# Backward of single-query attention on one core: scores as 512-column matmuls with q among 32 weights, and eight stores that leave out two DMA engines

## The chip, the core and the metric

The kernel runs on one core of one Trainium2 chip. The metric is the device time of one execution in microseconds, as the median of several runs; 1287.31 us before the change (five runs, 1287.27 to 1288.17). The profile shows one execution of the same program. The core has TensorE (PE, with its weight loads PEld), VectorE (DVE), ScalarE (ACT), GpSimd (POOL) and SyncE (SP), and sixteen DMA engines that all transfers share.

## The reference

For 64 heads (2 x 32), each with one query q of 128 numbers and 8,192 rows of k and v, all bf16, the reference computes the attention output and its gradients. In short, per head:

```
s  = (k . q) / sqrt(128)          8192 scores
p  = softmax(s)
out = p . v                        out_0
dp = v . grad_out                  8192
ds = p * (dp - sum(p * dp)) / sqrt(128)
dq = ds . k                        out_1
dk = ds outer q                    out_2, 8192 x 128
dv = p outer grad_out              out_3, 8192 x 128
```

So k and v of every head are read once (268 MB in all) and dk and dv are written once (268 MB). The scores of a head are 8,192 dot products with q for k, and as many with grad_out for v.

## The kernel before

**Tiles.** The k or the v of one head is one SBUF tile `kvt` of 2 MB: 128 partitions, each with NT = 64 rows of 128 numbers (16 KB per partition). There are NTILE = 12 such tiles, so six heads are in the core at a time. `outer` writes dk and dv over k and v in the same tile; the tile is stored from there, and when the store has landed, the load of the head six further on takes the place (`slot_of`, AHEAD = 6). Loads are issued from SP (`load`, L98), stores from POOL (L412, and L87 for the heads in SPREAD); only the last head is stored in four pieces per tile, from SP.

**Steps.** The main loop (L423) goes through steps of one chunk: 16 of the 64 rows per partition. A head has SL = 8 chunks, NCH = 4 of k and then 4 of v, and a new head begins every eight steps. The work of one head stretches over some 17 steps, so that up to three heads are in work at a time; `at(r)` and `within(r)` pick the head that stands at its step r. Every instruction is pinned (`pin`), so the order of the loop body is the order on each engine.

In a step, PE transposes the 16 blocks of the chunk with an identity into PSUM (L184, `tp`), and ACT copies them to SBUF (L186, `ev`). In the next step PE multiplies each transposed block as weights by the column q or grad_out (L195): sixteen matmuls with one moving column, each of which fills one column of `sw` (k) or `dpw` (v). That gives the scores with rows on the partitions. From there:

- r = 4: `max_part` takes the maximum per partition on DVE (L207); r = 5: `max_all` transposes it and reduces again (L211, L213); r = 6: `max_spread` brings it to all partitions (L218, L228), and `expo` computes the exponentials on ACT (L238); DVE casts them into `E_pad` (L247).
- r = 7: `normalise_p` sums (L282), takes the reciprocal and makes pairs of p (L291, L270, L295).
- r = 8: `weigh` computes the sum of p times dp (L253); r = 9: `normalise_ds` makes ds, `dS_pad` and its pairs (L305 to L270).
- r = 8 to 11 (`acc`, w = 1) and 12 to 15 (w = 0): p . v and ds . k as matmuls with 64 weights and 512 moving columns, in two halves of the array (L339); r = 12 and 16: `pick` (L356, L362) takes the wanted blocks out of the sum on DVE, and two steps later `join` adds them (L376, L379).
- r = 9 to 12 and 13 to 16: `outer` writes dv and dk, one chunk per step (L394, DVE); after the fourth chunk the tile is stored.

In steps r = 3 and r = 6, `broadcast` spreads grad_out and q over the partitions (L168 on PE, L177 on DVE).

**PSUM.** `sw` holds the scores of k, the transposed maximum and its broadcast; `dpw` holds those of v, two sums and the broadcast q (`qbp`). Each is one bank and there is one of each.

**Spread stores.** A store of 128 rows (one per partition) gives each of the sixteen DMA engines eight. The dk of the heads in SPREAD goes out as two stores instead, of 126 and of 2 rows (`by_rows`):

```python
SPREAD = range(5, 64, 9)
            if w == 0 and i in SPREAD:
                by_rows(store_eng, dst, h.tile[w], (P - 2, 2))
```

[...]

Of the kernel before, what the change touches and what calls it, by code (L numbers as in the profile page):

```python
# [11 lines left out]
BF16 = mybir.dt.bfloat16  # L12
F32 = mybir.dt.float32

CH = 16
QT = 4
CW = 64
NG = 2
NTILE = 12
FIRST = 6  # L20
SPREAD = range(5, 64, 9)


@with_exitstack
def kernel(
# [11 lines left out]
    nc = tc.nc  # L37
    B, H, Sq, D = q.shape
    Sk = k.shape[2]
    P = nc.NUM_PARTITIONS  # L40
    assert Sq == 1 and D == P
    BH = B * H
    assert BH <= P
    NT = Sk // P
    assert NT * P == Sk and NT % CH == 0
    NCH = NT // CH
    SL = 2 * NCH
# [4 lines left out]
    pin = tc.keep_in_program_order  # L52

    const = ctx.enter_context(tc.tile_pool(name="const", bufs=1))
    kvp = ctx.enter_context(tc.tile_pool(name="kv", bufs=1))
    evp = ctx.enter_context(tc.tile_pool(name="ev", bufs=2))
    work = ctx.enter_context(tc.tile_pool(name="work", bufs=1))
    small = ctx.enter_context(tc.tile_pool(name="small", bufs=2))
    ps_tp = ctx.enter_context(tc.tile_pool(name="ps_tp", bufs=2, space=bass.MemoryType.PSUM))
    ps_sdp = ctx.enter_context(tc.tile_pool(name="ps_sdp", bufs=1, space=bass.MemoryType.PSUM))  # L60
# [15 lines left out]
    heads = [Head() for _ in range(BH)]  # L76

    def slot_of(i, w):

        n = 2 * i + w  # L80
        return n if n < NTILE else slot_of(i - NTILE // 2, 1 - w)

    def by_rows(eng, dst, src, rows):

        p = 0
        for m in rows:
            pin(eng.dma_start(out=dst[p : p + m], in_=src[p : p + m], max_dma_last_dim=NT * D))  # L87
            p += m

    def load(i, w, pieces=(NCH,)):  # L90
        h = heads[i]
        t = kvp.tile([P, NT, D], BF16, tag=f"kv{slot_of(i, w)}", name="kvt")
        h.tile[w] = t
        src = (v_v if w else k_v)[i]
        c = 0
        for m in pieces:
            n0, n1 = c * CH, (c + m) * CH
            pin(load_eng.dma_start(out=t[:, n0:n1, :], in_=src[:, n0:n1, :]))  # L98
            c += m
# [4 lines left out]
    for w, a in enumerate((q, grad_out)):  # L104
        rows = a.rearrange("b h s d -> (b h s) d")
        r0 = FIRST if w == 0 else 0
        if r0:
# [3 lines left out]
                    out=qd_nat[:r0, w, :], in_=rows[:r0], max_dma_last_dim=D  # L111
# [4 lines left out]
    load(0, 1)  # L116
    for j in range(1, min(NTILE // 2, BH)):
        load(j, 0)
# [4 lines left out]
    ident_f = const.tile([P, P], F32)  # L123
    masks.make_identity(nc, ident_f[:])
    ones = const.tile([P, 1], F32)
    nc.vector.memset(ones[:], 1.0)
    groups = [g * P // NG for g in range(NG)]
    diag = const.tile([P, QT], F32)
# [7 lines left out]
    nc.vector.memset(E_pad[:], 0.0)  # L136
    nc.vector.memset(dS_pad[:], 0.0)

    qdT = const.tile([P, 2, BH], BF16)
    for w in range(2):  # L140
        tps = ps_m.tile([P, BH], BF16, tag=f"acc{w}", name="tps")
        nc.tensor.transpose(tps[:], qd_nat[:BH, w, :], ident_bf[:BH, :BH])
        nc.vector.tensor_copy(out=qdT[:, w, :], in_=tps[:])

    dqT = const.tile([P, BH], BF16)
    oT = const.tile([P, BH], BF16)

    def begin_s(i):

        h = heads[i]  # L150
        sw = ps_sdp.tile([P, NT + P + 1], F32, tag="s", name="sw")
        h.s = sw[:, 0:NT]
        h.mT = sw[0:1, NT : NT + P]
        h.mb = sw[:, NT + P :]

    def begin_dp(i):

        h = heads[i]
        dpw = ps_sdp.tile([P, NT + 2 + D], F32, tag="dp", name="dpw")
        h.dp = dpw[:, 0:NT]  # L160
        h.lsum = dpw[:, NT : NT + 2]
        h.qbp = dpw[:, NT + 2 :]

    def broadcast(i, w):

        h = heads[i]
        pin(
            nc.tensor.matmul(  # L168
                h.qbp,
                lhsT=qdT[:, w, i : i + 1].to_broadcast([P, P]),  # L170
                rhs=ident_bf[:],
                start=True,
                stop=True,
            )
        )
        h.qb[w] = small.tile([P, D], BF16, tag=f"qb{w}", name="qb")
        pin(nc.vector.tensor_copy(out=h.qb[w][:], in_=h.qbp))  # L177
# [9 lines left out]
        return ev  # L187

    def score_chunk(i, c, ev):
        h = heads[i]  # L190
        w, c = divmod(c, NCH)
        dst = h.dp if w else h.s
        for t in range(CH):
            pin(
                nc.tensor.matmul(  # L195
                    dst[:, c * CH + t : c * CH + t + 1],
                    lhsT=ev[:, t, :],
                    rhs=qdT[:, w, i : i + 1],
                    start=True,
                    stop=True,  # L200
                )
            )

    def max_part(i):
        h = heads[i]
        h.mp = small.tile([P, 1], F32, tag="mp", name="mp")
        pin(nc.vector.reduce_max(out=h.mp[:], in_=h.s, axis=AX.X))  # L207

    def max_all(i):
        h = heads[i]  # L210
        pin(nc.tensor.transpose(h.mT, h.mp[:], ident_f[:]))  # L211
        h.gm = small.tile([1, 1], F32, tag="gm", name="gm")
        pin(nc.vector.reduce_max(out=h.gm[:], in_=h.mT, axis=AX.X))  # L213
# [114 lines left out]
    def acc(i, w, c):  # L328
# [6 lines left out]
        for m in range(CH // QT):  # L335
            n0 = c * CH + m * QT
            g = groups[m % NG]
            pin(
# [3 lines left out]
                    rhs=rows[:, n0 : n0 + QT, :].rearrange("p n d -> p (n d)"),  # L342
                    start=(c == 0 and m < NG),
                    stop=(c == NCH - 1 and m >= CH // QT - NG),
                )
# [42 lines left out]
    def outer(i, w, c, ends):  # L388

        h = heads[i]  # L390
        n0 = c * CH
        shape = [P, CH, D // 2, 2]
        pin(
            nc.vector.tensor_tensor(  # L394
                out=h.tile[w][:, n0 : n0 + CH, :].rearrange("p n (e t) -> p n e t", t=2),
                in0=h.qb[w][:]
                .rearrange("p (e t) -> p e t", t=2)
                .unsqueeze(1)
                .to_broadcast(shape),
                in1=h.pair[w][:, n0 : n0 + CH, :].unsqueeze(2).to_broadcast(shape),  # L400
                op=ALU.mult,
            )
        )
        if c + 1 in ends:
            at = ends.index(c + 1)
            b0, b1 = (ends[at - 1] if at else 0) * CH, (c + 1) * CH
            dst = (dv_v if w else dk_v)[i]
            if w == 0 and i in SPREAD:
                by_rows(store_eng, dst, h.tile[w], (P - 2, 2))
            else:  # L410
                eng = load_eng if len(ends) > 1 else store_eng
                pin(eng.dma_start(out=dst[:, b0:b1, :], in_=h.tile[w][:, b0:b1, :]))  # L412
# [6 lines left out]
    last = list(range(1, NCH + 1))  # L419
    AHEAD = NTILE // 2  # L420

    prev = None
    for g in range(SL * BH + O0 + NCH + 4 - SL):  # L423
        now = [(g // SL - b, g % SL + b * SL) for b in range(4)]
        now = [(i, r) for i, r in now if 0 <= i < BH]

        def at(r0):

            return next((i for i, r in now if r == r0), None)

        def within(r0):

            return next(((i, r - r0) for i, r in now if r0 <= r < r0 + NCH), None)

        if (i := at(O1 + NCH)) is not None and i + AHEAD < BH:
            load(i + AHEAD, 0)
        if (i := at(O0 + NCH)) is not None and i + AHEAD < BH:
            load(i + AHEAD, 1)
        if x := within(O1):
            outer(x[0], 1, x[1], last if x[0] == BH - 1 else whole)  # L440
        if x := within(O0):
            outer(x[0], 0, x[1], last if x[0] == BH - 1 else whole)
        ev = None
        if g < SL * BH:
            i, r = divmod(g, SL)
            if r == 0:
                begin_s(i)
            if r == 3:
                begin_dp(i)
                broadcast(i, 1)  # L450
            if r == 6:
                broadcast(i, 0)
            ev = transpose_chunk(i, r)
        if (i := at(A1 + NCH + 2)) is not None:
            join(i, 1)
        if (i := at(A0 + NCH + 2)) is not None:
            join(i, 0)
        if x := within(A1):
            acc(x[0], 1, x[1])
        if x := within(A0):  # L460
            acc(x[0], 0, x[1])
        if (i := at(NCH + 2)) is not None:
            max_spread(i)
            expo(i)
        if prev is not None:
            score_chunk(*prev)
        prev = (g // SL, g % SL, ev) if ev is not None else None

        if (i := at(NCH)) is not None:
            max_part(i)  # L470
        if (i := at(NCH + 1)) is not None:
            max_all(i)
        if (i := at(NCH + 3)) is not None:
            normalise_p(i)
        if (i := at(SL)) is not None:
            weigh(i)
        if (i := at(SL + 1)) is not None:
            normalise_ds(i)
        if (i := at(A1 + NCH)) is not None:
            pick(i, 1)  # L480
        if (i := at(A0 + NCH)) is not None:
            pick(i, 0)

    for w, (src, dst) in enumerate(((dqT, out_1), (oT, out_0))):
        tps = ps_m.tile([BH, P], BF16, tag=f"acc{w}", name="tps")
# [34 lines left out]
```

## Time and profile before

| What | us |
|---|---|
| median of five runs | 1287.31 |
| the profiled execution, its own time | 1287.31 |
| its span, first to last instruction | 1285.5 |
| busy PE / PEld / DVE / ACT | 1127.2 / 857.7 / 935.7 / 975.9 |
| L195, matmuls of the scores, k / v: busy | 141.8 / 140.7 |
| L195, their weight loads: busy | 243.1 |
| L207, the maximum: idle of DVE before it | 152.2 |
| stores of 2,048 KB (POOL), issue to landing | 67.0 |
| loads of 2,048 KB (SP), issue to landing | 20.9 and 20.8 |
| mean granted clock of TensorE | 0.96 |

In the profile an engine's busy time is the union of its instructions; a matmul's end is modelled. Idle time stands before the group that followed it, with the instruction that ended most of it. DMA queue q1 is SP's, q0 POOL's, and q8 brings instructions. Read the queues as shares of the time of all sixteen DMA engines.

### The profile page before, as it was taken

Reading aid. Unit: us, or ns where it says so; the run is one execution under the profiler, and the core shown is the slowest. Engines: PE = TensorE matmul, PEld = TensorE weight load, DVE = VectorE, ACT = ScalarE, POOL = GpSimd, SP = SyncE. Lnnn points to the kernel's source line nnn. Section 1 sums busy time; section 2 is a strip of 40 time slices with the busy share of each in tenths; the row PEclk is TensorE's granted clock in tenths of the full one; section 3 lists DMA queues with packets and bytes.
Section 4 is the critical chain, followed back from the end, with each engine's and each line's share of the span. In section 5 each row is a group of like instructions: output and inputs, shape, how many; then the busy total and the mean of one; then the engine's idle time right before and its main releaser. Section 6 shows DMA issues by size and latency. Waiting matters only on the chain.

```text
span 1285.5 us, 42575 instructions
## 1 busy us (share of the span) xinstructions
PE 1127.2 (88%) x19268; PEld 857.7 (67%) x19268; DVE 935.7 (73%) x2122; ACT 975.9 (76%) x641; POOL 75.3 (6%) x142
## 2 busy tenths in 40 slices
PE   6999999988898988989888898889888998988880
PEld 5777777766676666766666676667666776766650
DVE  2888888777687777767776776768677777677781
ACT  6888888877787777877777787778777787777750
POOL 0000000000000000000000000000000000000000
PEclk9999999999999999999999899999899999899985
DMA  9999999999999999999999999999999999999995
GB/s 387 422 427 427 427 426 428 427 428 426 428 428 427 427 428 427 420 429 427 429 426 425 425 427 427 427 427 424 428 428 427 426 425 424 428 427 427 425 397 225
DMA packets 39986, 539.68 MB, mean 420 GB/s; under 512 B 5116, under 2 KB 5116, under 8 KB 6396
## 3 DMA queue, kind: packets, MB, share of 16 engines
q1 hardware_dynamic: 20172, 272.70, 49.9%
q0 software_dynamic: 19632, 264.25, 48.7%
q8 instruction: 150, 2.46, 0.7%
q14 instruction: 32, 0.26, 0.0%
HBM read 268.47 MB, written 268.47 MB: 418 GB/s over the span
## 4 chain that ended last, share of the span: by engine, by line
DMA 36%; PE 27%; another core or an unknown queue 19%; DVE 11%; issue 3%; ACT 1%; SPq 1%; POOL 0%; DVEq 0%; ACTq 0%; POOLq 0%
DMA kvt<-in_v_dram 26%; PE tp L184 12%; PE acc L339 7%; DVE kvt L394 6%; DMA kvt<-in_k_dram 5%; DMA out_dram<-kvt 4%; PE dpw L195 4%; PE sw L195 3%; DVE sel L362 2%; ACT ev L186 1%; PE dpw L282 1%; SPq L98 1%; DVE sel L356 1%; DMA qd_nat<-in_q_dram 1%
## 5 line engine op out<-in xcount | busy, mean ns | idle before, releaser
L186 ACT COPY ev<-tp 128x2048 bf16<-128x2048 bf16 x512 | 955.0, 1866 | 265.3 <-PE tp L184 253.6
L184 PE MATMUL tp<-ident_bf,kvt 128*128 128x128 bf16 x8192 | 557.3, 223 | 95.9 <-DMA kvt<-in_v_dram 73.9
L394 DVE TENSOR_TENSOR kvt<-qb,pair 128x2048 bf16<-128x2048 bf16 x512 | 621.9, 1215 | 0.2
L184 PEld LDWEIGHTS <-kvt 128*128 128x128 bf16 x8192 | 488.8, 100 | 102.6 <-DMA kvt<-in_v_dram 77.6
L195 PEld LDWEIGHTS <-ev 128*128 128x128 bf16 x8192 | 243.1, 96 | 208.2 <-issue 148.9
L339 PE MATMUL acc<-kvt,dS_pad 128*64 128x512 bf16 x1024 | 167.4, 409 | 0.8 <-DVE dqT L379 0.8
L339 PE MATMUL acc<-kvt,E_pad 128*64 128x512 bf16 x1024 | 160.5, 394 | 0.0
L195 PE MATMUL dpw<-qdT,ev 128*128 128x1 bf16 x4096 | 140.7, 164 | 17.8 <-DVE qb L177 17.0
L362 DVE SCALAR_TENSOR_TENSOR sel<-acc,diag,sel 128x128 f32<-128x128 f32 x384 | 134.7, 351 | 13.6
L195 PE MATMUL sw<-qdT,ev 128*128 128x1 bf16 x4096 | 141.8, 164 | 1.2 <-ACT ev L186 1.2
L412 POOL DMA_DIRECT2D out_dram<-kvt x119 | 64.0, 537 | 1089.4 <-DVE kvt L394 984.5
L207 DVE TENSOR_REDUCE mp<-sw 128x1 f32<-128x64 f32 x64 | 14.4, 225 | 152.2 <-PE sw L195 152.2
L339 PEld LDWEIGHTS <-dS_pad 128*64 128x64 bf16 x1024 | 37.5, 110 | 24.4 <-issue 5.1
L247 DVE CAST E_pad<-E_f 128x64 bf16<-128x64 f32 x64 | 12.5, 196 | 55.4 <-ACT E_f L238 55.4
L339 PEld LDWEIGHTS <-E_pad 128*64 128x64 bf16 x1024 | 36.4, 108 | 21.3 <-issue 0.7
L376 PE MATMUL acc<-ones,sel 128*128 128x1 f32 x256 | 43.5, 239 | 6.2 <-DVE sel L362 6.2
L253 DVE CUSTOM_DVE_ANT_0 junk<-E_f,dpw 128x64 bf16<-128x64 f32 x64 | 14.2, 221 | 45.5 <-PE dpw L195 45.5
L282 PE MATMUL dpw<-ld,ones 128*128 128x1 f32 x256 | 46.3, 250 | 0.1
L356 DVE TENSOR_SCALAR sel<-acc,diag 128x128 f32<-128x128 f32 x128 | 44.2, 345 | 0.0
L376 PEld LDWEIGHTS acc<-ones,sel 128*128 128x128 f32 x256 | 39.2, 194 | 7.3 <-DVE sel L362 7.3
L177 DVE CAST qb<-dpw 128x128 bf16<-128x128 f32 x128 | 35.6, 278 | 6.2 <-PE dpw L168 6.2
L282 PEld LDWEIGHTS dpw<-ld,ones 128*128 128x128 f32 x256 | 38.2, 188 | 0.5 <-DVE ld L253 0.5
(44 smaller groups left out, 313.5 us busy)
## 6 DMA issues: line engine op xcount, KB each, us to landing
out_dram<-kvt POOLq DMA_DIRECT2D x119, 2048.0 KB, 67.0
kvt<-in_v_dram SPq DMA_DIRECT2D x64, 2048.0 KB, 20.9
kvt<-in_k_dram SPq DMA_DIRECT2D x63, 2048.0 KB, 20.8
out_dram<-kvt POOLq DMA_DIRECT2D x7, 2016.0 KB, 70.3
out_dram<-kvt SPq DMA_DIRECT2D x8, 512.0 KB, 24.1
kvt<-in_k_dram SPq DMA_DIRECT2D x2, 512.0 KB, 4.5
kvt<-in_k_dram SPq DMA_DIRECT2D x1, 1024.0 KB, 7.1
out_dram<-kvt POOLq DMA_DIRECT2D x7, 32.0 KB, 70.3
```

Source lines behind the costliest of these rows:

```text
L177: pin(nc.vector.tensor_copy(out=h.qb[w][:], in_=h.qbp))
L184: pin(nc.tensor.transpose(tp[:, t, :], src[:, c * CH + t, :], ident_bf[:]))
L186: pin(nc.scalar.copy(out=ev[:], in_=tp[:]))
L195: nc.tensor.matmul(dst[:, c * CH + t : c * CH + t + 1], lhsT=ev[:, t, :], rhs=qdT[:, w, i : i + 1], start=True, stop=True,)
L207: pin(nc.vector.reduce_max(out=h.mp[:], in_=h.s, axis=AX.X))
L282: nc.tensor.matmul(out, lhsT=ones[:].to_broadcast([P, P]), rhs=col, start=True, stop=True)
L339: nc.tensor.matmul(h.acc[w][g : g + CW, :], lhsT=wts[:, n0 : n0 + CW], rhs=rows[:, n0 : n0 + QT, :].rearrange("p n d -> p (n d)"), start=( ...
L356: nc.vector.tensor_scalar(out=h.sel[:], in0=block, scalar1=diag[:, 0:1], scalar2=None, op0=ALU.mult)
L362: nc.vector.scalar_tensor_tensor(out=h.sel[:], in0=block, scalar=diag[:, b : b + 1], in1=h.sel[:], op0=ALU.mult, op1=ALU.add,)
L376: nc.tensor.matmul(h.acc[w][:, 0:1], lhsT=h.sel[:], rhs=ones[:], start=True, stop=True)
L394: nc.vector.tensor_tensor(out=h.tile[w][:, n0 : n0 + CH, :].rearrange("p n (e t) -> p n e t", t=2), in0=h.qb[w][:] .rearrange("p (e t) -> ...
L412: pin(eng.dma_start(out=dst[:, b0:b1, :], in_=h.tile[w][:, b0:b1, :]))
```

## The change

Two edits.

**Spread stores.** SPREAD goes from seven heads (5, 14, ... 59) to eight (4, 11, ... 53).

**Scores.** The transposed chunk `ev` becomes the moving operand, and q a column among 32 weights. q and grad_out of head i stand in `qdT` at column Q0 + 4i, with zeros between; chunk c takes the 32 columns that begin c before it, so that q is weight c of the 32 and the others are zero. Four matmuls of 512 columns, one for each quarter of the array's columns, write four groups of 32 partitions of a new PSUM tile `raw`; the four chunks of k (then of v) are added up in it, so that partition 32g + c holds the scores of quarter g of chunk c. `keep_raw` copies `raw` to SBUF on DVE, and `spread_rows` brings the scores back to rows on partitions with four fp32 matmuls by a selection `sel4`. `sw` and `dpw` become one tile, in one bank. max_part, max_all, max_spread, expo, normalise_p, weigh and normalise_ds stand one step later than before; acc, outer, pick, join, loads and stores keep their steps. broadcast of grad_out goes from r = 3 to r = 4.

```diff
-SPREAD = range(5, 64, 9)
+SG = 4
+SW = 32
+SPREAD = range(4, 60, 7)
...
+    sel4 = const.tile([P, NCH, SG], F32)
+    nc.vector.memset(sel4[:], 0.0)
+    for g in range(SG):
+        nc.vector.tensor_copy(
+            out=sel4[g * SW : (g + 1) * SW, :, g],
+            in_=ident_f[g * SW : (g + 1) * SW, g * SW : g * SW + NCH],
+        )
+
+    Q0 = NCH - 1
+    qdT = const.tile([P, 2, Q0 + NCH * BH + SW], BF16)
+    nc.vector.memset(qdT[:], 0.0)
...
-    def begin_s(i):
...
-    def begin_dp(i):
...
+    def begin(i):
+
+        h = heads[i]
+        sw = ps_sdp.tile([P, 2 * NT + 2 * P + 4], F32, tag="s", name="sw")
+        h.score = (sw[:, 0:NT], sw[:, NT : 2 * NT])
+        h.s, h.dp = h.score
...
     def score_chunk(i, c, ev):
+
         h = heads[i]
         w, c = divmod(c, NCH)
-        dst = h.dp if w else h.s
-        for t in range(CH):
+        if c == 0:
+            h.raw = ps_sdp.tile([P, QT * P], F32, tag="raw", name="raw")
+        q0 = Q0 + NCH * i - c
+        for g in range(SG):
             pin(
                 nc.tensor.matmul(
-                    dst[:, c * CH + t : c * CH + t + 1],
-                    lhsT=ev[:, t, :],
-                    rhs=qdT[:, w, i : i + 1],
+                    h.raw[g * SW : (g + 1) * SW, :],
+                    lhsT=qdT[:, w, q0 : q0 + SW],
+                    rhs=ev[:, g * QT : (g + 1) * QT, :].rearrange("p n d -> p (n d)"),
+                    start=(c == 0),
+                    stop=(c == NCH - 1),
+                )
+            )
+
+    def keep_raw(i):
+
+        h = heads[i]
+        h.rows = work.tile([P, QT * P], F32, tag="rows", name="rows")
+        pin(nc.vector.tensor_copy(out=h.rows[:], in_=h.raw[:]))
+
+    def spread_rows(i, w):
+
+        h = heads[i]
+        for t in range(QT):
+            pin(
+                nc.tensor.matmul(
+                    h.score[w].rearrange("p (n t) -> p n t", t=QT)[:, :, t],
+                    lhsT=h.rows[:, t * P : (t + 1) * P],
+                    rhs=sel4[:].rearrange("p c g -> p (c g)"),
                     start=True,
                     stop=True,
                 )
...
-            if r == 0:
-                begin_s(i)
-            if r == 3:
-                begin_dp(i)
+            if r == NCH:
+                begin(i)
                 broadcast(i, 1)
-            if r == 6:
+            if r == NCH + 2:
                 broadcast(i, 0)
...
-        if (i := at(NCH + 2)) is not None:
+        if (i := at(NCH + 1)) is not None:
+            spread_rows(i, 0)
+        if (i := at(SL + 1)) is not None:
+            spread_rows(i, 1)
+        if (i := at(NCH + 3)) is not None:
             max_spread(i)
             expo(i)
...
         if (i := at(NCH)) is not None:
+            keep_raw(i)
+        if (i := at(SL)) is not None:
+            keep_raw(i)
+        if (i := at(NCH + 1)) is not None:
             max_part(i)
-        if (i := at(NCH + 1)) is not None:
+        if (i := at(NCH + 2)) is not None:
             max_all(i)
-        if (i := at(NCH + 3)) is not None:
+        if (i := at(NCH + 4)) is not None:
             normalise_p(i)
-        if (i := at(SL)) is not None:
+        if (i := at(SL + 1)) is not None:
             weigh(i)
-        if (i := at(SL + 1)) is not None:
+        if (i := at(SL + 2)) is not None:
             normalise_ds(i)
```

In the changed kernel the lines stand some 30 further down: L178 and L187 are broadcast's two, L194 and L196 the transposes and their copy, L208 the scores, L221 keep_raw, L228 spread_rows, L240 max_part, L280 the cast to E_pad, L315 the sum, L372 acc, L395 pick's last, L427 outer.

More of the change, by code (lines that the diff above doesn't have):

```diff
@@ L137 @@
     nc.vector.memset(dS_pad[:], 0.0)
-    qdT = const.tile([P, 2, BH], BF16)
+    sel4 = const.tile([P, NCH, SG], F32)
[8 more added lines that the diff above has]
+    nc.vector.memset(qdT[:], 0.0)
     for w in range(2):
@@ L142 @@
         nc.tensor.transpose(tps[:], qd_nat[:BH, w, :], ident_bf[:BH, :BH])
-        nc.vector.tensor_copy(out=qdT[:, w, :], in_=tps[:])
+        nc.vector.tensor_copy(
+            out=qdT[:, w, Q0 : Q0 + NCH * BH].rearrange("p (i f) -> p i f", f=NCH)[:, :, 0],
+            in_=tps[:],
+        )
     dqT = const.tile([P, BH], BF16)
     oT = const.tile([P, BH], BF16)
-    def begin_s(i):
+    def begin(i):
         h = heads[i]
[L151 to L154, printed above, removed]
-    def begin_dp(i):
[L158 to L162, printed above, removed]
+        sw = ps_sdp.tile([P, 2 * NT + 2 * P + 4], F32, tag="s", name="sw")
+        h.score = (sw[:, 0:NT], sw[:, NT : 2 * NT])
+        h.s, h.dp = h.score
+        h.mT = sw[0:1, 2 * NT : 2 * NT + P]
+        h.qbp = sw[:, 2 * NT + P : 2 * NT + 2 * P]
+        h.lsum = sw[:, 2 * NT + 2 * P : 2 * NT + 2 * P + 2]
+        h.mb = sw[:, 2 * NT + 2 * P + 2 : 2 * NT + 2 * P + 3]
     def broadcast(i, w):
@@ L169, in broadcast @@
                 h.qbp,
-                lhsT=qdT[:, w, i : i + 1].to_broadcast([P, P]),
+                lhsT=qdT[:, w, Q0 + NCH * i : Q0 + NCH * i + 1].to_broadcast([P, P]),
                 rhs=ident_bf[:],
@@ L191, in score_chunk @@
         w, c = divmod(c, NCH)
-        dst = h.dp if w else h.s
-        for t in range(CH):
+        if c == 0:
+            h.raw = ps_sdp.tile([P, QT * P], F32, tag="raw", name="raw")
+        q0 = Q0 + NCH * i - c
+        for g in range(SG):
             pin(
                 nc.tensor.matmul(
-                    dst[:, c * CH + t : c * CH + t + 1],
-                    lhsT=ev[:, t, :],
-                    rhs=qdT[:, w, i : i + 1],
+                    h.raw[g * SW : (g + 1) * SW, :],
[4 more added lines that the diff above has]
+                )
+            )
+    def keep_raw(i):
[10 more added lines that the diff above has]
+                    rhs=sel4[:].rearrange("p c g -> p (c g)"),
                     start=True,
```

## The prediction

> **What bounds the kernel now.** I read the page first: its engine shares, its DMA strip and its queue table.
>
> ```profile
> span 1285.5 us, 42575 instructions
> ...
> PE 1127.2 (88%) x19268; PEld 857.7 (67%) x19268; DVE 935.7 (73%) x2122; ACT 975.9 (76%) x641; POOL 75.3 (6%) x142
> ...
> DMA  9999999999999999999999999999999999999995
> ...
> q1 hardware_dynamic: 20172, 272.70, 49.9%
> q0 software_dynamic: 19632, 264.25, 48.7%
> q8 instruction: 150, 2.46, 0.7%
> ```
>
> No compute engine is full, and the DMA engines are: 49.9 + 48.7 + 0.7 is 99.3% of sixteen engines' span. The loss is at the end. Next, the table of stages (columns: window, PE, PEld, DVE, ACT, POOL, granted clock, DMA share, GB/s):
>
> ```profile
> 60.00:260.00 200.00, 194.66 (x3442) 149.34 (x3441) 167.11 (x381) 173.88 (x115) 13.15 (x24) 1.00 1.01 427
> 280.00:1220.00 940.00, 837.17 (x14288) 636.42 (x14285) 693.47 (x1566) 723.82 (x475) 56.06 (x101) 0.97 1.01 427
> 1256.00:1285.00 29.00, 0.90 (x3) 0.63 (x3) 1.97 (x8) 0.00 (x0) 0.00 (x0) 0.50 0.51 213
> ```
>
> Three stages. Up to 260 us PE is 97% busy: there data is ahead, and the heads follow each other at compute's own pace. From 280 us the pace is DMA's. After 1256 us nothing computes, and half of the DMA engines' time still runs. The waits of PE in the middle stage confirm it:
>
> ```profile
> PE tp L184 <- DMA kvt<-in_v_dram: 69.8, 39, 4.7
> PE tp L184 <- DMA kvt<-in_k_dram: 20.7, 24, 2.0
> PE dpw L195 <- DVE qb L177: 12.0, 38, 0.3
> ```
>
> The landing events show who is late. The last 512 KB store (issued at 1255.0 us) has sixteen, one per engine: seven between 1258.7 and 1259.8, two at 1269.3 and 1271.2, seven between 1277.6 and 1282.5. The packet records carry no engine number, but a 16 KB row takes 611 ns and the next packet of that engine starts 4 ns before it ends, so I chained them from 20 to 780 us. Eight of the sixteen chains hold 11 to 13 instruction packets each, the others one at most. One further chain has rows about 5% longer. At a spread store two chains take one row where the others take nine: one that holds instruction packets, and the 5% one. An instruction packet lasts 0.98 us and stretches the row behind it by some 0.3, so 1.3 in all; 150/8 x 1.3 = 24 us, which is the lateness of the last seven. So **seven engines that fetch instructions and are not relieved set the end**, without idle time until then.
>
> Compute's own pace, from the starts of the first transpose of each chunk of head 10: 2.18, 2.18, 1.95, 1.95, 2.12, 2.81, 2.18, 1.95, together 17.32 us per head. DMA needs (1285.5 - 10)/64 = 19.9. Compute has 2.6 us per head to spare.
>
> [...] in acc (128x64) the matmuls of a pair start 3 ns apart, the second pair 0.24 us later, the next mode 0.31 after that. Four 128x32 tiles no trace here shows. [...] The records show 256 packets of 8,192 B per such store.
>
> **The change, part by part.**
>
> *Instruction fetch.* 38,536 PE records and 2.46 MB make 64 B each. Removed: 16,384 (8,192 loads and matmuls of L195). Added: 512 x 4 loads and matmuls of scores, 4,096; 64 x 2 x 4 fp32 spreads, which run as two passes with a load each as L376's 256 for 128 calls do, 2,048. Left 28,296, so 110 packets, 40 fewer, 5 per fetching engine: **-6.5 us** on each.
>
> *Spread stores.* Eight for seven: engines 4 and 5 save 7 more rows (-4.3 us); the other fourteen get one more, **+0.6 us**, the seven late ones included. The relieved ones were not last, so the saving is worth nothing. Moving them from heads 5..59 to 4..53 shifts work in queues that are full anyway; their DMA issue (0.69 us each on POOL) lies in POOL's 1,089 us idle. Without that cover it would be 1.4 us per store.
>
> DMA-bound end: 1285.5 - 6.5 + 0.6 = **1279.6 us** of span.
>
> *Scores on PE.* Sixteen N=1 matmuls hold PE 0.40 us per chunk (25 ns apart). Four 512-column ones in four tiles: 0.24 if they overlap[...]. As pairs overlap fully in acc, I take 0.33: a plain step goes from 1.95 to 1.88. ACT needs 1.87 + 0.03 for its copy, so it becomes 1.9.
>
> *keep_raw and spread_rows.* keep_raw is 128x512 fp32 from PSUM. [...] so I take 0.68[...]. 128 of them add 87 us to DVE, 73% to 80%. spread_rows: eight fp32 passes 0.11 apart (the spacing in L282), 0.89 plus one more mode change: +0.97 us of PE, twice per head.
>
> *Moved by one step:* max_part, max_all, max_spread, expo, normalise_p, weigh, normalise_ds; acc and outer stay. Two waits follow.
> - In the program's order the broadcast of q at r = 6 now stands in the bank of the scores and waits for max_part. From the first transpose of r = 5: transposes 1.04, acc 0.55, spread and switch 0.95, scores 0.33, so PE is ready at 2.87. DVE: keep_raw to 0.70, pick (0.38 + 2 x 0.39 + 0.27) to 2.1, outer to 3.25, max_part to 3.48. Step r = 5 is about 3.6: **+0.7**. Queued behind it are the next transposes, and ACT's copy behind those. The old qb wait (0.3) goes.
> - E_pad is cast one step before acc reads it instead of two. From the transposes of r = 7: these end at 1.05, copy 1.87, expo 0.5, cast 0.2 and hand-overs: 3.7; PE would be there at 2.12 + 1.04 = 3.15: **+0.55**. Behind it wait acc, the scores and ev's release.
>
> Laid out so, in program order with the durations above, the steps are: r0 2.7, r1 2.8, r2 2.25, r3 1.9, r4 1.9, r5 3.6, r6 2.15, r7 2.1 = 19.4. The same layout of the old order gives 17.24 against 17.32 measured, so **19.5 us per head**, against 17.32.
>
> Is that still under DMA? The first dk store is issued at 44.6 us now; with the slower steps some 3 later: 47.7. 63 x 19.5 more is 1276, less 7 because the last nine steps have no transposes: the last chunk store at 1269. The end follows 7 to 9 us after (last join, final transposes, two row stores; 1263.4 against 1256.1 today, and a landing of 2): 1277. DMA's 1279.6 ends last, by little. [...] I add 1. The profiled execution took 1287.31 for its span of 1285.5, 1.8 around it, and equals the median. **1280.6 + 1.8 = 1282.5 us.**
>
> *Start:* the extra memsets and five small copies on DVE run before 9.2 us, when qd_nat lands; DVE idles there. Uncovered, about 1 us.
>
> **The rivals.**
> - *Compute becomes the bound (slower).* Each 0.1 us per head is 6.4 us. From 19.6 per head the end passes today's; at 20.0 it is about 1312, at 20.4 about 1338. For it: my margin is half a per cent; four tiles 20 ns apart would already cost 0.3 per head; no trace shows the mode. Against: pairs overlap to 3 ns, and waits on PE let DVE catch up. [...]
> - *No measurable difference.* 19.6 per head, or the fetch packets saved are not those of the engines that end last: then only the spread's +0.6 is left. 1287 to 1288. Against: eight chains carry the fetches, one of them is relieved, and seven engines end last.
> - *A full gain:* pace at or under 19.2, the end purely DMA's: 1281.4, or 1279 if the late engines' other stretched rows shrink too. Same side as the forecast.
>
> **How the numbers follow.** A measurement of this kernel tells 0.2%, 2.6 us, from no change. Forecast and full gain: 50%, 1279 to 1284.7; no difference 13%; compute-bound 37%, spreading as far as the pace does (19.6 to 20.4). Range: below 1279 nothing but rounding; at the top the compute-bound case is cut at a pace of 20.0. 1279 to 1311; the forecast's own range is 1280 to 1285.
>
> **What would show it.** q8: about 110 packets. Landings of the last big store: late group some 6 us nearer to the early one. Chunk steps up to 260 us: 19.5 per head, with PE waiting for mp before L178 and for E_pad before L372. DMA at 9 in every slice and PE still waiting on kvt: DMA-bound. DMA share under 1 and no PE wait on kvt: rival one. keep_raw at 0.68, score matmuls within 15 ns of each other. I am wrong if the tiles run one after the other, or if one more wait of half a microsecond per head sits on PE.

## The result and the profile after

The changed kernel takes **1281.01 us** (median of 26 executions, 1279.6 to 1288.1) where the kernel before, run beside it, takes 1288.17 (47 executions). The ratio is 0.9944, with a 95% interval from 0.9932 to 0.9955: 7.2 us faster. The forecast was 1282.5. The profiled execution took 1279.41 us, with a span of 1277.6.

The page of the changed kernel, lines that answer to those shown of the kernel before:

```profile
span 1277.6 us, 32473 instructions
...
PE 1191.0 (93%) x14148; PEld 810.6 (63%) x14148; DVE 1025.9 (80%) x2256; ACT 975.8 (76%) x641; POOL 76.2 (6%) x143
...
DMA  9999999999999999999999999999999999999997
...
q8 instruction: 110, 1.80, 0.5%
```

PE has 5,120 matmuls fewer and yet 64 us more of busy time: the instructions that went were tiny (128x1, 25 ns apart), and those that came are large (128x512, 391 ns each). Instruction packets fell from 150 to 110. The DMA engines are as full as before, and the last slice is now busier (7 for 5). The table of stages (window, PE, PEld, DVE, ACT, POOL, granted clock, DMA share, GB/s):

```profile
60.00:260.00 200.00, 190.02 (x2273) 129.05 (x2270) 162.84 (x358) 157.23 (x105) 11.55 (x21) 1.00 1.01 428
280.00:1220.00 940.00, 893.64 (x10690) 608.92 (x10689) 773.00 (x1698) 735.77 (x484) 57.13 (x103) 1.00 1.01 427
1256.00:1285.00 29.00, 8.12 (x33) 3.36 (x33) 12.65 (x27) 0.00 (x0) 0.00 (x0) 0.59 0.53 216
```

Both middle stages now have the same PE share, 95%, at a full clock. The waits of PE between 280 and 1220 us say why (waiting line, what it waits for, us in total, times, longest us):

```profile
PE sw L178 <- DVE mp L240: 29.1, 48, 0.8
...
PE acc L372 <- DVE E_pad L280: 17.2, 48, 0.4
```

These are the two waits that the prediction named, and in that stage PE has none for `kvt`, where the kernel before waited 90.5 us for it. So from the fourth head to the sixtieth the heads follow each other at compute's own pace: 19.44 us each. The timeline of PE shows one head of it (start, us, line, instructions; in brackets the idle time ahead and what ended it):

```profile
397.87 0.62 PE L372 MATMUL acc<-kvt,E_pad 128*64 128x512 bf16 x4
398.42 1.06 PE L228 MATMUL sw<-sel,rows 128*128 128x16 f32 x8
399.42 0.40 PE L208 MATMUL raw<-ev,qdT 128*32 128x512 bf16 x4
399.75 1.07 PE L194 MATMUL tp<-ident_bf,kvt 128*128 128x128 bf16 x16
...
409.40 0.22 PE L178 MATMUL sw<-ident_bf,qdT 128*128 128x128 bf16 x1 [0.60 <-DVE mp L240]
...
415.20 0.62 PE L372 MATMUL acc<-kvt,E_pad 128*64 128x512 bf16 x4 [0.36 <-DVE E_pad L280]
```

From spread_rows (398.42) to the scores is 1.00 us, from the scores (399.42) to the next transposes 0.33. The four score matmuls of a chunk start 3 or 4 ns apart in the records, so the four tiles do overlap.

The landing events of the last but one 512 KB store show the end. (It is issued at 1266.0, and its counterpart in the kernel before at 1255.0; the prediction calls that one the last, but one more was issued at 1256.1, here at 1267.1.) Nine DMA engines land between 1268.6 and 1269.4, the other seven from 1271.1 to 1274.6. In the kernel before the last seven landed from 1277.6 to 1282.5, so they are 6.5 to 7.8 us earlier now. They were up to 24 us behind the first; now it is 6, because the first, too, comes 10 us later, with the later issue. The page's chain of the work that ended last is 61% PE and 4% DMA. So two things that look opposed are both in this trace: nothing computing waits for data, and some DMA engines are still late at the end. Which of the two sets the time was the open question.

### The profile page after: what moved, and what is told of

Its sections match the earlier page's. It is cut to its first block, busy times and chain, and to the rows that moved or that the text cites. A ratio compares the mean times of both kernels' runs of the same rounds, so it can differ in the third digit from the quotient of the medians.

```text
span 1277.6 us, 32473 instructions
## 1 busy us (share of the span) xinstructions
PE 1191.0 (93%) x14148; PEld 810.6 (63%) x14148; DVE 1025.9 (80%) x2256; ACT 975.8 (76%) x641; POOL 76.2 (6%) x143
## 4 chain that ended last, share of the span: by engine, by line
PE 61%; DVE 16%; ACT 11%; issue 7%; DMA 4%; POOL 0%; ACTq 0%; SPq 0%; POOLq 0%; DVEq 0%
PE tp L194 25%; PE acc L372 15%; ACT ev L196 9%; PE raw L208 9%; DVE kvt L427 6%; PE sw L228 5%; DMA out_dram<-kvt 4%; DVE sel L395 4%; DVE rows L221 3%; PE sw L315 3%; PE sw L178 2%; PE acc L409 2%; ACT E_f L271 1%; DVE sel L389 1%; DVE E_pad L280 1%
## 5 line engine op out<-in xcount | busy, mean ns | idle before, releaser
L196 ACT COPY ev<-tp 128x2048 bf16<-128x2048 bf16 x512 | 955.0, 1867 | 274.5 <-PE tp L194 268.0
L427 DVE TENSOR_TENSOR kvt<-qb,pair 128x2048 bf16<-128x2048 bf16 x512 | 617.2, 1216 | 0.2
L194 PE MATMUL tp<-ident_bf,kvt 128*128 128x128 bf16 x8192 | 543.8, 219 | 0.0
L194 PEld LDWEIGHTS <-kvt 128*128 128x128 bf16 x8192 | 481.8, 99 | 81.3 <-issue 80.4
L208 PE MATMUL raw<-ev,qdT 128*32 128x512 bf16 x2048 | 205.2, 391 | 1.6 <-ACT ev L196 1.6
L372 PE MATMUL acc<-kvt,E_pad 128*64 128x512 bf16 x1024 | 160.7, 394 | 24.5 <-DVE E_pad L280 24.5
L372 PE MATMUL acc<-kvt,dS_pad 128*64 128x512 bf16 x1024 | 160.7, 395 | 0.0
L228 PEld LDWEIGHTS sw<-sel,rows 128*128 128x128 f32 x1024 | 124.7, 192 | 52.7 <-DVE sel L395 25.9
L395 DVE SCALAR_TENSOR_TENSOR sel<-acc,diag,sel 128x128 f32<-128x128 f32 x384 | 134.8, 351 | 13.6
L208 PEld LDWEIGHTS <-qdT 128*32 128x32 bf16 x2048 | 53.1, 93 | 136.6 <-issue 131.8
L228 PE MATMUL sw<-sel,rows 128*128 128x16 f32 x1024 | 137.1, 266 | 0.0
L221 DVE COPY rows<-raw 128x512 f32<-128x512 f32 x128 | 88.6, 692 | 22.5 <-PE raw L208 22.4
L280 DVE CAST E_pad<-E_f 128x64 bf16<-128x64 f32 x64 | 12.5, 195 | 80.4 <-ACT E_f L271 80.4
L372 PEld LDWEIGHTS <-E_pad 128*64 128x64 bf16 x1024 | 36.2, 108 | 49.9 <-DVE E_pad L280 35.7
L178 PE MATMUL sw<-ident_bf,qdT 128*128 128x128 bf16 x128 | 28.5, 223 | 38.2 <-DVE mp L240 38.2
L246 DVE TENSOR_REDUCE gm<-sw 1x1 f32<-1x128 f32 x64 | 17.8, 278 | 55.4 <-PE sw L244 55.4
L315 PEld LDWEIGHTS sw<-ld,ones 128*128 128x128 f32 x256 | 38.3, 189 | 29.9 <-issue 15.2
L372 PEld LDWEIGHTS <-dS_pad 128*64 128x64 bf16 x1024 | 36.6, 108 | 22.3 <-issue 1.0
L315 PE MATMUL sw<-ld,ones 128*128 128x1 f32 x256 | 49.3, 262 | 0.0
## 6 DMA issues: line engine op xcount, KB each, us to landing
kvt<-in_v_dram SPq DMA_DIRECT2D x64, 2048.0 KB, 19.4
kvt<-in_k_dram SPq DMA_DIRECT2D x63, 2048.0 KB, 19.5
```

Of the source, the lines that this page charges most:

```text
L194: pin(nc.tensor.transpose(tp[:, t, :], src[:, c * CH + t, :], ident_bf[:]))
L196: pin(nc.scalar.copy(out=ev[:], in_=tp[:]))
L208: nc.tensor.matmul(h.raw[g * SW : (g + 1) * SW, :], lhsT=qdT[:, w, q0 : q0 + SW], rhs=ev[:, g * QT : (g + 1) * QT, :].rearrange("p n d -> ...
L221: pin(nc.vector.tensor_copy(out=h.rows[:], in_=h.raw[:]))
L228: nc.tensor.matmul(h.score[w].rearrange("p (n t) -> p n t", t=QT)[:, :, t], lhsT=h.rows[:, t * P : (t + 1) * P], rhs=sel4[:].rearrange("p ...
L315: nc.tensor.matmul(out, lhsT=ones[:].to_broadcast([P, P]), rhs=col, start=True, stop=True)
```

## The experiments

My theory on seeing these views was that compute sets the end of the changed kernel, DMA's own limit lying just below it. The rival was the sum of my prediction, in which DMA ends last by 2.6 us. A second question was whether the 7 us came from the instruction packets at all, and a third what the stores are worth.

### What the gain is made of: stores or instruction packets

The kernel before with the eight stores alone:

```diff
-SPREAD = range(5, 64, 9)
+SPREAD = range(4, 60, 7)
```

> The kernel before with the eight stores of 126 + 2 rows (heads 4 to 53) and nothing else. My theory: the seven engines that fetch instructions and are not relieved set its end; they get one row more (0.6 us), and the relieved two were not last. Time +0.6 us, ratio 1.000 to 1.001; the last 512 KB store's late seven landings stay 22 to 24 us behind the early ones. Rival (the relieved engines 4 and 5 hold up the loads that compute waits for, and so set the pace): 7 rows less for them are worth up to 4.3 us, ratio 0.997.

Measured: 1287.24 us against 1288.42, ratio 0.999 (0.998 to 1.0001). Between 2.6 us gained and nothing. Neither side is hit squarely: the loss of 0.6 us is just outside the interval, the gain of 4.3 well outside. In the landings of the same store the late seven stood 18.1 to 19.4 us behind the first in this execution, less than the 22 to 24 expected; the two in the middle moved from 10.6 and 12.5 us to 5.2 and 9.1. The records carry no engine number, so 4 and 5 are mere names for the two relieved engines.

The changed kernel with the old seven stores, so the scores alone:

```diff
-SPREAD = range(4, 60, 7)
+SPREAD = range(5, 64, 9)
```

> The changed kernel with the seven stores of 126 + 2 rows that the kernel before had (heads 5 to 59): the scores alone. My theory (compute sets the end, DMA just below it): the stores are worth nothing either way, within 0.1% of the changed kernel, 1280 to 1282. Rival (the relieved engines 4 and 5, or the place of the last spread store at head 53 in place of 59, matter now that the other engines are less late): 1283 to 1285.

Measured: 1280.33 us, ratio 0.9951 (0.9934 to 0.9969), the whole change again. The stores carry none of the gain that can be measured.

Next, the kernel before with fewer instructions and nothing else changed in its work for DVE, ACT or DMA. It multiplies one block in four, by the columns of four heads at once, and so leaves twelve of a chunk's sixteen blocks out of the scores:

```diff
-        for t in range(CH):
+        j = min(i, BH - 4)
+        for t in range(0, CH, 4):
...
-                    dst[:, c * CH + t : c * CH + t + 1],
+                    dst[:, c * CH + t : c * CH + t + 4],
...
-                    rhs=qdT[:, w, i : i + 1],
+                    rhs=qdT[:, w, j : j + 4],
```

> The kernel before, with four matmuls of four columns per chunk in place of sixteen of one column (the columns of four heads' q are taken, so the scores of k and v are wrong and their block assignment too; every other instruction is the same). That takes 12 x 512 x 2 = 12,288 PE records, 0.79 MB, 48 instruction packets off and shortens PE, which is not the bound there. My theory (instruction packets on the late seven engines, 1.3 us each, 6 per engine): -7.8 us, about 1280, q8 at 102 packets, the late landings of the last 512 KB store 15 to 17 us behind the early ones. Rival (fetching costs the late engines nothing, and their lateness comes from elsewhere): no change, 1287 to 1288, lateness still 24 us. A second rival (each costs more than I priced, 1.6 us, as the changed kernel's landings suggest): -9.6 us.

Measured: 1279.60 us against 1288.42, ratio 0.9939 (0.9925 to 0.9952): 8.8 us less, where 7.8 was expected. Its page has the packets:

```profile
q8 instruction: 102, 1.67, 0.5%
```

The other sign that I expected did not come: the last landing is 25.9 us behind the first, not 15 to 17, because the early engines land sooner here too (the first at 1249.6 for 1258.7). The last seven landed from 1270.6 to 1275.5, 7 us earlier than in the kernel before.

This kernel also computes faster (15.45 us per head), so the gain could have come from there. To tell these apart, the same kernel was padded on PE with two long matmuls per chunk that cost time and few instructions:

```diff
+        for t in (4, 8):
+            pin(
+                nc.tensor.matmul(
+                    h.idle[w],
+                    lhsT=ev[:, t, :],
+                    rhs=ev[:, t : t + 3, :].rearrange("p n d -> p (n d)")[:, 0:312],
+                    start=True,
+                    stop=True,
+                )
+            )
```

> The kernel before with four matmuls of four columns per chunk (scores wrong in the same way as in the run with a quarter of the score matmuls), and two more of 312 columns into unused columns of the same bank, which nobody reads. They bring compute's own pace from 15.45 back to about 17.4 us per head, that of the kernel before (17.32), while instructions stay away: of the 12 matmuls saved per chunk two come back, so 10 x 512 x 2 = 10,240 records, 40 packets fewer than before, as many as the change saves. My theory (the packets of instructions on the late engines, 1.3 us each, 5 per engine): -6.5 us, 1281 to 1282. Rival (the shorter matmuls made the gain of the run before, by letting chunks through sooner): no gain, 1288.

Measured: 1281.86 us against 1288.23, ratio 0.995 (0.9933 to 0.9968): **6.4 us less for 40 packets**. The pace up to 180 us was 16.92 us per head, near the 17.32 of the kernel before. Its page and, below, its waits from 280 to 1220 us:

```profile
q8 instruction: 110, 1.80, 0.5%
```

```profile
PE tp L186 <- DMA kvt<-in_v_dram: 80.3, 41, 6.3
...
PE tp L186 <- DMA kvt<-in_k_dram: 25.0, 30, 1.5
```

PE waits for data here as much as in the kernel before (105 us for 90.5), and still the end came 6 us sooner (4 to 9 by the interval). The packets and bytes of the other queues are those of the kernel before, and the last seven landings came at 1270.8 to 1277.4, 5 to 7 us earlier. So packets of instructions are the gain: 40 of them are worth, within the scatter, what the whole change brought. That they are five on each of eight engines rests on the prediction's chaining of packets; no run here counts them for each engine.

### Which of compute and DMA ends last in the changed kernel

Faster compute first. q's broadcast goes two steps earlier, into PSUM columns that the transposed maximum uses later, so that PE has nothing to wait for:

```diff
+        h.qbq = sw[:, 2 * NT : 2 * NT + P]
...
+        dst = h.qbp if w else h.qbq
...
-                h.qbp,
+                dst,
...
             if r == NCH:
                 begin(i)
                 broadcast(i, 1)
-            if r == NCH + 2:
                 broadcast(i, 0)
+                keep_qb(i, 1)
+                keep_qb(i, 0)
```

> The changed kernel with q's broadcast two steps earlier, beside that of grad_out, into the columns of the bank that the transposed maximum uses later; so PE no longer waits for max_part there. My theory (in the changed kernel compute sets the end, DMA's own end lies just below): step r5 falls from 3.6 to about 3.0 us, the pace up to 260 us from 19.45 to about 18.9 us per head; after that PE waits for kvt again and DMA sets the pace; the last big store's landings spread to more than 6 us; time 1276 to 1279, ratio to the kernel before 0.990 to 0.993. Rival (DMA sets the changed kernel's end already, by 2.6 us as in my sum): waits for kvt take the place of the wait for max_part, 1281, no change from the changed kernel. Rival (compute alone, DMA has room): 64 x 0.6 = 38 us less, 1243.

Measured: 1285.79 us (1278.9 to 1296.5), ratio 0.9978 (0.9961 to 0.9995). Step r5 fell to 2.88 us and the pace to 18.79, and none of these 63 x 0.65 = 41 us showed up in the time. The waits of PE from 280 to 1220 us:

```profile
PE tp L200 <- DMA kvt<-in_v_dram: 16.8, 18, 3.5
PE acc L378 <- DVE E_pad L286: 12.8, 36, 0.4
PE tp L200 <- DMA kvt<-in_k_dram: 9.2, 13, 0.9
```

The wait for mp is gone and the wait for `kvt` is back. Up to 730 us the heads follow each other every 18.79 us, so the faster compute uses up the data that lies ahead, and then DMA sets the pace. That the median was even 4 to 5 us above the changed kernel I had not foreseen, so the run was repeated for a second profile and then timed beside the changed kernel.

> The changed kernel with q's broadcast two steps earlier, again, for a second profile: its executions lay between 1279 and 1297 us, and the profiled one was the shortest. My theory: in a longer one compute is unchanged (18.8 us per head until PE first waits for kvt), and one or more DMA engines run later, so that the last big store's landings spread over more than 19 us. Rival: compute is slower somewhere (a longer step than 18.8 us per head ahead of the first wait for kvt).

Measured: 1280.38 us. The execution was again a short one, with 18.79 us per head and a spread of 19.2 us at the end, so it doesn't answer the question.

> The changed kernel with q's broadcast two steps earlier, timed again beside the changed kernel itself. If being bound by DMA costs it something by itself, it stays 3 to 5 us above the changed kernel and scatters more (1279 to 1297 the first time). If that was chance of the first series, the two agree within 1 us.

> The changed kernel as it is, beside its variants: 1280 to 1282 if its first series holds.

Measured side by side: 1282.40 us for the early broadcast, ratio 0.9955 (0.9943 to 0.9967), and 1282.48 for the changed kernel, 0.9958 (0.9942 to 0.9973). They agree; the difference of the first series does not hold up. That series and this pair ran on two different chips, so a difference between chips is not excluded.

The other wait is taken away by putting the first acc of p . v behind the scores of its step:

```diff
-        if x := within(A1):
-            acc(x[0], 1, x[1])
+        x1 = within(A1)
+        if x1 and x1[1]:
+            acc(x1[0], 1, x1[1])
...
             score_chunk(*prev)
+        if x1 and not x1[1]:
+            acc(x1[0], 1, 0)
```

> The changed kernel with the first acc of p . v (r = 8) behind the scores of that step in place of ahead of them, so that E_pad has 0.35 us more; the wait for max_part stays. Steps r7 and r0 should lose about 0.3 us together, pace 19.1 to 19.2. My theory (19.45 is paced by compute, DMA's own limit is reached near 19.2 to 19.3 on average, beyond which the end only moves over to the late DMA engines): 1279 to 1284, no gain against the changed kernel that can be measured, PE waiting for kvt late in the run. Rival (compute alone): 63 x 0.3 = 19 us less, 1262.

Measured: 1279.38 us, ratio 0.994 (0.9925 to 0.9954). The pace is 19.12, and the time that of the changed kernel.

Both edits together:

> The changed kernel with both waits taken away: q's broadcast two steps earlier, and the first acc behind the scores. My theory: pace 18.4 to 18.5 us per head up to about 260 us, after which DMA sets the pace as in the run with the broadcast alone; PE waits more for kvt, no gain, 1280 to 1286. Rival (what made the broadcast's run 4 us longer than the changed kernel belongs to the broadcast's new place): here it is again, the same 1284 to 1288. Rival (running deeper into DMA's limit is itself dear): longer than the broadcast alone, over 1288.

Measured: 1281.64 us, ratio 0.996 (0.9944 to 0.9976), at a pace of 18.46; PE waits 41.1 us for `kvt` from 280 to 1220 us. The profiled execution was a longer one, with a span of 1285.2 us. Of the landings of its last 512 KB store fourteen came within 10.2 us of the first and one at 11.0; a single one was 19.9 us behind. So in this execution one DMA engine alone made the difference. Why it was late no run here shows.

Now slower compute. Four transposes per head are done twice, in a step that PE bounds:

```diff
-        for t in range(CH):
+        for t in (*range(CH), *(range(4) if (w, c) == (0, 1) else ())):
             pin(nc.tensor.transpose(tp[:, t, :], src[:, c * CH + t, :], ident_bf[:]))
```

> The changed kernel with four of the sixteen transposes of each head's second chunk done twice (256 instructions more on PE in all, in a step that PE bounds). No wait grows by it, so TensorE's clock should stay at full, unlike in the run with 128 columns copied twice. My theory (compute sets the end): 4 x 55 ns = 0.22 us per head, pace 19.66, 63 x 0.22 = 13.9 us more, 1294 to 1296, ratio 1.004 to 1.006. Rival (DMA ends last by 2.6 us, as in my sum): 11 us, 1292. Rival (every slowing of compute is dear, as in that other run, where 0.33 us per head cost 59): about 40 us, 1320.

Measured: 1289.84 us, ratio 1.0013 (1.0001 to 1.0025), which is 7.4 us above the changed kernel timed beside it and 8.8 above its first series. The pace is 19.67, exactly as expected, TensorE's mean granted clock is 0.993 (0.990 in the changed kernel's profile), and the waits are the old ones:

```profile
PE sw L178 <- DVE mp L240: 28.5, 47, 0.8
PE acc L372 <- DVE E_pad L280: 17.1, 48, 0.4
```

But the time grew by less than the 13.9 us of my theory. The landings tell where the rest went. The last 512 KB store was issued at 1281.0 us, 13.9 later than at 1267.1, so compute did end 13.9 later. Its sixteen landings came within 0.8 us of each other: the late engines had caught up. In the changed kernel's profile the span went on for 7.0 us after the issue of the last row store (1270.6 to 1277.6), here for 3.2 (1284.6 to 1287.8). So **in the changed kernel the late DMA engines end 3.8 us after compute would**, and in the medians by 13.9 - 8.8 = 5.1 or 13.9 - 7.4 = 6.5 us. My theory of compute as the end falls; the rival, the prediction's own sum with 2.6 us (11 us for this run), came nearer, and the margin is larger still. The scatter agrees: the executions of the changed kernel lie 8.5 us apart, those of this one 1.9 us (1289.3 to 1291.2), as if nothing were left of the DMA engines' own scatter once compute ends last.

The other way to slow compute was on DVE, ahead of the maximum for which PE waits:

```diff
         pin(nc.vector.tensor_copy(out=h.rows[:], in_=h.raw[:]))
+        if first:
+            pin(nc.vector.tensor_copy(out=h.rows[:, 0:P], in_=h.raw[:, 0:P]))
```

> The changed kernel with 128 columns of raw copied a second time on DVE at r = 4 (0.28 us, 64 times), ahead of max_part, for which PE waits. My theory (compute sets the end throughout): step r5 grows by 0.28, the pace to 19.73, and the time by 63 x 0.28 = 17.6 us to 1298 or 1299, ratio to the kernel before about 1.008 to 1.009. Rival (my prediction's sum, in which DMA ends last by 2.6 us and compute has that much to spare): 15 us, 1296. Rival (DMA sets the end, with the slack that the faster variant seems to show): under 10 us more.

Measured: 1340.58 us, ratio 1.0408 (1.0385 to 1.0431): 59.6 us above the changed kernel, and no theory had that. Step r5 is 3.93 us, 0.33 more than 3.60, which makes 21 us. The rest is in the timeline of PE:

```profile
426.46 0.40 PE L208 MATMUL raw<-ev,qdT 128*32 128x512 bf16 x4
427.78 0.22 PE L178 MATMUL sw<-ident_bf,qdT 128*128 128x128 bf16 x1 [0.93 <-DVE mp L242]
427.84 1.81 PE L194 MATMUL tp<-ident_bf,kvt 128*128 128x128 bf16 x16
...
429.90 1.07 PE L374 MATMUL acc<-kvt,dS_pad 128*64 128x512 bf16 x4
...
431.54 1.06 PE L194 MATMUL tp<-ident_bf,kvt 128*128 128x128 bf16 x16
```

After a wait of 0.93 us the transposes take 1.81 us in place of 1.06 and acc 1.07 in place of 0.62; the next transposes are back at 1.06. TensorE ran at half speed in between. The clock records of this kernel have 28 such stretches between 50 and 1310 us, of 3.41 us each; the changed kernel, with its wait of 0.6 us at the same place, has none up to 1250 us. A head with such a stretch takes 21.3 us, one without 19.77. So 28 x 1.5 is 42 us, and 42 + 21 makes 63. The last row store was issued 63.9 us later (1334.55 for 1270.64), the span grew by 60.1 (1277.6 to 1337.7), and the difference is again the 3.8 us by which DMA ended after compute. The table of stages carries it (granted clock 0.96 from 280 to 1220 us, DMA share and GB/s behind it):

```profile
280.00:1220.00 940.00, 880.77 (x10149) 596.68 (x10145) 747.01 (x1656) 699.52 (x461) 54.51 (x98) 0.96 1.00 415
```

### All paces together

| variant | us per head while nothing waits for data | median us |
|---|---|---|
| both waits taken away | 18.46 | 1281.64 |
| q's broadcast early | 18.79 | 1285.79, then 1282.40 |
| first acc behind the scores | 19.12 | 1279.38 |
| the changed kernel | 19.44 | 1281.01, then 1282.48 |
| four transposes twice | 19.67 | 1289.84 |
| 128 columns copied twice | 19.77, and 21.3 where the clock drops | 1340.58 |

One us per head, or 63 us, lies between the first and the fourth row, and the time does not follow it. From there on it does. No variant beats the changed kernel by more than the scatter.

## Why the prediction was right

- **Instruction packets, -6.5 us: shown.** 40 packets taken off the kernel before by themselves brought 6.4 us, 48 brought 8.8 where 1.3 us each gave 7.8. That is 1.27 and 1.47 us for a packet on a late engine, if eight engines share them evenly.
- **Spread stores, +0.6 us on the late seven: not confirmed in sign**, and too small to matter. Alone they measured -1.2 us, with an interval that ends at +0.1. That the relief of the other two engines is worth nothing holds: 4.3 us would have shown.
- **Scores on PE, 0.33 us a chunk: right.** It was my estimate from the trace of before: 0.24 us from one pair of acc to the next, and 0.09 us for the change of the tile shape ahead of acc, whose first matmul starts 149 ns after the last transpose, where transposes start 55 ns apart. That four tiles overlap as two do was not shown before the change; they do, with starts 3 or 4 ns apart. spread_rows took 1.00 us for 0.97. keep_raw took 692 ns; the 680 for it was my estimate, which no trace of before shows.
- **The two waits: right in place, a bit too large.** For mp 0.61 us (29.1 in 48) for my 0.7, for E_pad 0.36 (17.2 in 48) for my 0.55. The first is of a kind that the kernel before shows for `qb` (12.0 us in 38): a matmul into a PSUM tile behind a read of that tile on DVE.
- **The steps.** Predicted r0 to r7: 2.7, 2.8, 2.25, 1.9, 1.9, 3.6, 2.15, 2.1. Measured: 2.55, 2.86, 2.29, 1.94, 1.87, 3.60, 2.15, 2.18, together 19.44 for 19.4, or 19.5 with the calibration. The last chunk store was issued at 1267.1 for my 1269.
- **DMA ends last, by little: right**, though I doubted it on seeing the trace. The run with four transposes twice puts the margin at 3.8 us in the profiles; the sum had 1279.6 against 1277. Both ends lie lower than I had them, DMA's at 1277.6 and compute's at 1273.8 (1277.6 less the margin).
- **The mis-sized terms** are these two ends, and the 1 us added to them, a guess that rests on no trace. The forecast was 1.5 us too high. As a difference it was too small: 4.8 us less than the 1287.31 that I started from, where the two kernels run side by side differ by 7.2. The +0.6 for the spread stores and this +1, neither of which was found, are 1.6 of these 2.4 us. That the time came out closer than the difference is luck: over 47 executions the kernel before takes 0.9 us more than the median of five that I had.
- **The list of signs had a gap.** I had written that PE still waiting for `kvt` would mean DMA, and no such wait together with a DMA share under 1 would mean compute. What came was a full DMA share and no wait. With six heads in the core, data that lay ahead at the start lasted for the whole run: a load landed 34 us ahead of its first transpose at 404 us, and 15 us ahead at 1192 us. Loads came later and later without ever being late, and only the last stores showed it. These 19 us over 40 heads make 0.5 us per head, so an estimate of DMA's own pace from them is 19.44 + 0.5 = 19.9, the figure that the prediction began with. The sign at the landings missed too: the late group came 18 us nearer to the early one, not some 6. It landed 6.5 to 7.8 us earlier, and the early group, of which the prediction says nothing, 10 us later.
- **The compute-bound rival** was priced at 6.4 us for each 0.1 us per head. On PE alone that is right (13.9 us for 0.22, of which DMA hid 4 to 6.5). Where the 0.1 us is a wait of PE it can be far dearer, as where the clock dropped (with 128 columns copied twice 0.33 us per head went with 59.6 us, at a granted clock of 0.96 from 280 to 1220 us): the upper end of my range had that cost nowhere.

## What to carry to other kernels

When the DMA engines are full, count the instructions as bytes too, and ask which engines carry them: 10,240 PE records taken away were worth 6 us here, although PE was nowhere near the bound. A new stage may cost compute all its slack (here 2.1 of 2.6 us per head) and still be a gain, but then the next fifth of a microsecond per head is paid for (0.22 us with 7.4 to 8.8 us). Absence of waits for data (none from 280 to 1220 us here) doesn't show that DMA isn't the end (3.8 us after compute here): look at the landings of the last stores and at how far ahead of their use the loads land, and slow compute by a known amount to see how much of it arrives.

## What was not expected of the hardware

In the run with 128 columns copied twice TensorE went to half speed for stretches of 3.41 us after waits of 0.93 us that came once per head; after the waits at the same place in the changed kernel, 0.61 us on average and 0.8 at most from 280 to 1220 us, it did not. In the run with the stretches no wait of PE from 280 to 1220 us was longer than 0.93 us, so no longer one was needed for them.

The clock records also show which heads were hit. The starts of the 28 stretches lie whole multiples of 3.413 us apart. By the instruction records there are 62 waits of 0.92 or 0.93 us between 50 and 1310 us: 34 fall whole into one interval of this grid, and 28 of these were followed by a stretch at the grid's next point; the other 28 waits are cut by a grid point, and none was. Yet the length of a wait does not decide alone. With q's broadcast early, longer waits passed without a stretch, as this one:

```profile
732.91 1.07 PE L200 MATMUL tp<-ident_bf,kvt 128*128 128x128 bf16 x16 [2.85 <-DMA kvt<-in_v_dram]
```

A grid point cuts this one too, at 731.2, but that leaves 1.7 us of it in one interval. The work beside the wait differs between the two places; what it is that counts no run here shows.
